# Seven of twelve weight pieces of the second mixer decoded inside its first block, with the pieces in another order

## The chip, the core and the metric

The kernel runs on one core of a Trainium2 chip. The metric is the device time of one execution in microseconds (us). The engines are PE (TensorE, matmuls), PEld (its weight loads), DVE (VectorE), ACT (ScalarE), POOL (GpSimd) and SP (SyncE, which issues the DMAs here). Each runs its own queue in order.

## What is computed

The reference is three steps one after the other. B = 4 sequences, S = 768 positions, 8 heads of 48 (together 384 columns).

```python
# linear attention with a decaying state, per head
for t in range(S):
    cur = einsum('bhd,bhe->bhde', u * k[t], v[t])
    y[t] = einsum('bhd,bhde->bhe', r[t], state + cur)
    state = w * state + einsum('bhd,bhe->bhde', k[t], v[t])
# first mixer: 384 -> 1024 -> 384, a convolution of 3 taps makes the gate
h = maximum(x @ w_in, 0)
conv = conv_w[0] * h[t-1] + conv_w[1] * h[t] + conv_w[2] * h[t+1]
x = (h * sigmoid(conv)) @ w_out
# second mixer: 384 -> 1536 -> 384, with a norm ahead and a residual
xn = (x - mean) / sqrt(var + 1e-6) * g_ln
out = x + maximum(xn @ w_ch1, 0) @ w_ch2
```

## The kernel before

All rows are cut into 24 tiles of 128. Attention makes one tile after the other (generator `attention`, two steps a tile). The first mixer runs in 8 blocks of 384 rows (loop variable j, 0 to 7), each over 8 slices f of 128 of the 1024 inner columns. The second mixer runs in 6 blocks of 512 rows, each over 12 slices f of the 1536. In a slice 9 matmuls make `psm` from the three column groups of the input (high x high, high x low, low x high part of input and weight), and the products with the second matrix go into accumulators `acc`, 9 or 12 matmuls, three slices late (`LAG`). The second mixer takes `rh` (ACT, line 487) and `rl` (DVE, line 488) out of psm, which has two buffers. In the first mixer DVE makes `c` (lines 474 and 455) and `gl` (line 461), and for attention `rk`, `kks`, `av`, `a`, `aT`, `sn`, `sw` and `xl`. Attention's steps are put between the slices by a count, `pace`.

**Weight pieces.** Weights come as words that must be decoded into a high and a low part. A piece is 128 rows by 768 (or 512) columns; `wjob` (line 139) makes a job of it. There are 22 jobs: 0 to 9 are the first mixer's weights, 10 to 21 the second mixer's: six pieces of `w_ch1` (`c1h`, `c1l`, three for each half of 768 columns) and six of `w_ch2` (`c2h`, `c2l`, each for two slices f). A job loads `st` (SP, three buffers), takes the magnitude into `wdec` (ACT, line 75 in the profile) and clamps it (POOL), then has four steps on DVE: a shift, two merges with `st` (SCALAR_TENSOR_TENSOR wdec<-st,wdec), and the low part `c1l` or `c2l`, which needs ACT's copy `c1h` or `c2h`. All these helpers stand at line 75 in the profile. `wdo(count, last)` (line 208) takes that many steps; the fourth step of a job and the first of the next go together, so a job takes three counts. `need(job)` finishes all jobs up to that one.

**What sets the order.** The loops call `wdo` at fixed places: `after1` (line 768) runs twice a slice of the first mixer, `after2` (line 798) once a slice of the second. The jobs run in the order of their making. The program order is then changed by a scheduler that works ahead of time and keeps, on each engine, the decode and all matmuls in program order but may move the others around them. `before2` calls `need` for the pieces which the slice uses. `choose_path` (line 713) loads w and makes a flag `general` on DVE; line 811 reads the flag into a register on every engine.

Of the kernel before, what the change touches and what calls it, by code (L numbers as in the profile page):

```python
# [16 lines left out]
DM = H * D  # L17
# [4 lines left out]
NF2 = FF2 // 128  # L22
# [9 lines left out]
NB = B * BPB  # L32
# [16 lines left out]
def body(ctx, tc, r, k, v, w, u, w_in, conv_w, w_out, g_ln, w_ch1, w_ch2, rkT, krv, small, out):  # L49
# [59 lines left out]
    c2h = [big.tile([128, 2, DM], F32R, name=f"c2h{f}") for f in range(NF2 // 2)]  # L109
    c2l = [big.tile([128, 2, DM], F32R, name=f"c2l{f}") for f in range(NF2 // 2)]  # L110
# [8 lines left out]
    def magnitude(st, n, engine=go):  # L119

        t = ap.tile([128, WN], F32, tag="wd", name="wdec", bufs=2)[:, 0:n]
        ao.activation(out=t, in_=words(st, n)[1].bitcast(F32), func=AF.Abs)
        engine.tensor_scalar(out=t, in0=t, scalar1=W_MIN, scalar2=W_MAX, op0=ALU.max, op1=ALU.min)
        return t
# [14 lines left out]
    def wjob(src, n, hi, lo, scale=None):  # L139

        st, mag = [], []

        def load():
            st.append(io.tile([128, 2 * WN], I32, tag="st", name="st", bufs=3))
            dst = st[0][:, 0:2 * n]
            if len(src.shape) == 3:
                dst = dst.rearrange("p (a n) -> p a n", a=src.shape[1])
            so.dma_start(out=dst, in_=src.bitcast(I32))

        def ahead():  # L150
            if not mag:
                mag.append(magnitude(st[0], n, vo if me < 4 else go))

        def steps():
            ahead()
            t = mag[0]
            yield from decode(st[0], n, t)
            if me + 1 < min(len(wjobs), w_loaded[0]):
                wjobs[me + 1][2]()
            if len(src.shape) == 3:  # L160
                t = t.rearrange("p (a n) -> p a n", a=src.shape[1])
            kw = {} if scale is None else {"scale": gl[:, scale:scale + 1]}
            ao.activation(out=hi, in_=t, func=AF.Copy, **kw)
            yield
            if scale is None:
                vo.tensor_tensor(out=lo, in0=t, in1=hi.bitcast(F32), op=ALU.subtract)
            else:
                vo.scalar_tensor_tensor(out=lo, in0=t, scalar=kw["scale"], in1=hi.bitcast(F32),
                                        op0=ALU.mult, op1=ALU.subtract)
        me = len(wjobs)  # L170
        wjobs.append((load, steps(), ahead))
        return len(wjobs) - 1

    wi_job, wo_job, c1_job, c2_job = {}, {}, {}, {}

    def rows2(w_, f):
        return w_[f * 128:f * 128 + 256, :].rearrange("(a p) d -> p a d", p=128)
# [14 lines left out]
    for f0 in range(0, FF2, WN):  # L192
        for kt in range(KT):
            for f in range(f0 // 128, (f0 + WN) // 128):
                c1_job[f] = len(wjobs)
            wjob(w_ch1[kt * 128:kt * 128 + 128, f0:f0 + WN], WN, c1h[f0 // WN][kt],
                  c1l[f0 // WN][kt], kt)
    for f in range(0, NF2, 2):
        c2_job[f] = c2_job[f + 1] = wjob(rows2(w_ch2, f), 2 * DM, c2h[f // 2], c2l[f // 2])
    w_loaded, w_done = [0], [0]  # L200

    def wload(count):
# [5 lines left out]
    def wdo(count=1, last=None):  # L208

        for _ in range(count):  # L210
            while w_done[0] < (len(wjobs) if last is None else last + 1):
                wload(w_done[0] + 2)
                if next(wjobs[w_done[0]][1], "end") != "end":
                    break
                w_done[0] += 1
# [541 lines left out]
    for j in range(NB):  # L757
        slot = [0]
        while finished[0] < min((j + 1) * TT - (j % 2), NT - 1):
            step()  # L760

        def before1(f):
            if f < NF1:
                need(wi_job[f // 4])
            if f >= LAG - 1:
                need(wo_job[f - LAG + 1])

        def after1(f):
            slot[0] += 1
            pace[0] += 2 if j else 1.9  # L770
            if j == 1:
                pace[0] += 0.4
            if pace[0] >= 5:
                pace[0] -= 5
                step()
            if j == 0:
                wdo(2, wo_job[NF1 - 1])
            elif j < NB - 2:
                wdo(slot[0] % 4 == 0, c1_job[NF2 - 1])
            else:  # L780
                wdo(slot[0] % 3 == 0, c2_job[4])
            if j == NB - 1:
                if slot[0] == 1:
                    ahead[0] = prefetch(0)
                elif slot[0] >= 7:
                    next(ahead[0], None)

        mixer1(xT[j], spill(j), before1, after1)
# [4 lines left out]
    for j in range(NB2):  # L793
        def before2(f):
            need(c1_job[f])
            need(c2_job[max(f - LAG + 1, 0)])

        def after2(f):
            wdo(2)
            if f == 1 and j + 1 < NB2:  # L800
                ahead[0] = prefetch(j + 1)
            elif f >= 4:
                next(ahead[0], None)

        x1s, xn = normed.pop(j)
        mixer2(xn, TT2, lambda acc, x1s=x1s, j=j: finish(
            acc, x1s, lambda t0: rows[j * T2 + t0:j * T2 + t0 + 128, :]), before2, after2)
        for _ in ahead[0]:
            pass
# [70 lines left out]
```

## Time and profile before

| what | value |
|---|---|
| timed runs | 675.46 us median of 3 (673.67 to 676.84) |
| the profiled execution | 671.88 us, span 670.2 us, mean granted clock 0.977 |
| PE busy | 630.2 us, 94% of the span |
| DVE busy | 426.6 us, 64% |
| ACT busy | 263.5 us, 39% |
| POOL busy | 133.8 us, 20% |
| start of the second mixer's first psm | 352.48 us |
| start of the last matmul | 664.04 us |

Times in the profile count from the start of the span. The share of an engine is a mean over the whole span. Waits name what ended last before the waiting instruction could start. The granted clock is a share of TensorE's 2.4 GHz; its other level is 1.2 GHz. A block of the second mixer takes some 50 us.

### The profile page before, as it was taken

How to read it: one execution, taken by the hardware profiler on the slowest of the kernel's cores; microseconds unless marked ns; L12 is line 12 of the kernel's file. 1: busy time of each engine (PE TensorE's matmuls, PEld its weight loads, DVE VectorE, ACT ScalarE, POOL GpSimd, SP SyncE). 2: the span in 40 equal slices, each digit the busy share in tenths (PEclk: the TensorE clock that was granted, in tenths of full speed). 3: DMA queues.
4: the chain of work that ended last, by engine and by line, in shares of the span. 5: the costliest groups of instructions: out<-in, count | busy, mean ns of one | idle time of the engine just before them, and what ended most of it. 6: DMA issues, size and time to landing. Idle time of an engine off the chain costs nothing.

```text
span 670.2 us, 11679 instructions
## 1 busy us (share of the span) xinstructions
PE 630.2 (94%) x4782; PEld 574.5 (86%) x4782; DVE 426.6 (64%) x772; ACT 263.5 (39%) x518; POOL 133.8 (20%) x142
## 2 busy tenths in 40 slices
PE   5979799989899999999999999999999999999996
PEld 4858678879788888999998999999999999999996
DVE  7869999989998999977999522412422422421211
ACT  3457566546464565566774311221111221121110
POOL 6466532312031213211415000100100100100000
PEclk9988899989899998999999999999999999999998
DMA  8655525245235433203043002000200200200101
GB/s 281 193 170 189 176 76 183 85 149 166 78 110 176 141 107 128 84 2 130 5 140 118 0 1 70 25 1 27 68 1 23 72 1 13 83 1 1 47 1 51
DMA packets 25294, 56.50 MB, mean 84 GB/s; under 512 B 2961, under 2 KB 15378, under 8 KB 25234
## 3 DMA queue, kind: packets, MB, share of 16 engines
q1 hardware_dynamic: 25234, 55.68, 26.2%
q8 instruction: 39, 0.64, 0.4%
q14 instruction: 21, 0.17, 0.1%
HBM read 46.24 MB, written 9.44 MB: 83 GB/s over the span
## 4 chain that ended last, share of the span: by engine, by line
PE 67%; DVE 18%; DMA 6%; issue 4%; POOL 2%; ACT 2%; SPq 0%; DVEq 0%; POOLq 0%
PE acc L75 30%; PE psm L75 30%; DMA rk<-in_rkT_dram 5%; DVE c L474 4%; DVE wdec L75 4%; PE yps L75 3%; DVE rk L347 3%; PE dps L75 1%; DVE aT L363 1%; DVE gl L461 1%; DVE c L455 1%; PE pxt L75 1%; POOL wdec L75 1%; DMA x1b<-x_dram 1%; PE pst L75 0%
## 5 line engine op out<-in xcount | busy, mean ns | idle before, releaser
L488 DVE SCALAR_TENSOR_TENSOR rl<-psm,rh 128x512 fp32r<-128x512 f32 x72 | 49.5, 688 | 141.2 <-ACT rh L487 141.2
L487 ACT ACTIVATE rh<-psm 128x512 fp32r<-128x512 f32 x72 | 43.1, 598 | 202.6 <-PE psm L75 202.6
L75 PE MATMUL acc<-c2l,rh 128*128 128x384 f32 x288 | 97.1, 337 | 0.0
L75 PE MATMUL acc<-c2h,rl 128*128 128x384 f32 x288 | 97.0, 337 | 0.0
L75 PE MATMUL acc<-c2h,rh 128*128 128x384 f32 x288 | 96.9, 336 | 0.0
L75 PE MATMUL psm<-xnh,c1h 128*128 128x512 f32 x216 | 86.6, 401 | 0.0
L474 DVE SCALAR_TENSOR_TENSOR c<-h,tables,c 128x384 f32<-128x384 f32 x128 | 83.9, 661 | 3.8 <-ACT c L472 3.2
L75 PE MATMUL psm<-xnh,c1l 128*128 128x512 f32 x216 | 85.0, 394 | 0.0
L75 PE MATMUL psm<-xnl,c1h 128*128 128x512 f32 x216 | 84.7, 392 | 0.0
L75 PE MATMUL acc<-woh,gl 128*128 128x384 f32 x192 | 66.8, 348 | 7.5 <-DVE gl L461 7.5
L75 PE MATMUL psm<-xh,wih 128*128 128x386 f32 x192 | 69.0, 359 | 4.1 <-DVE aT L363 2.7
L75 PE MATMUL acc<-wol,gh 128*128 128x384 f32 x192 | 66.0, 344 | 3.9 <-DVE wol L75 3.9
L75 PE MATMUL acc<-woh,gh 128*128 128x384 f32 x192 | 68.0, 354 | 1.4 <-ACT x L496 1.3
L75 PE MATMUL psm<-xl,wih 128*128 128x386 f32 x192 | 67.0, 349 | 2.4 <-POOL xl L288 2.4
L75 PE MATMUL psm<-xh,wil 128*128 128x386 f32 x192 | 67.2, 350 | 1.7 <-DVE wil L75 1.7
L75 POOL TENSOR_SCALAR wdec<-wdec 128x768 f32<-128x768 f32 (+2 forms) x19 | 53.7, 2825 | 74.7 <-ACT wdec L75 70.1
L511 POOL TENSOR_TENSOR rs<-rs,nhalf 128x1 f32<-128x1 f32 x24 | 18.4, 772 | 214.1 <-DVE rs L510 201.7
L75 PEld LDWEIGHTS acc<-c2l,rh 128*128 128x128 f32 x288 | 54.1, 188 | 3.0
L75 PEld LDWEIGHTS acc<-c2h,rh 128*128 128x128 f32 x288 | 54.1, 188 | 2.8
L75 PEld LDWEIGHTS acc<-c2h,rl 128*128 128x128 f32 x288 | 54.1, 188 | 0.0
L460 ACT ACTIVATE gh<-c 128x384 fp32r<-128x384 f32 x64 | 33.3, 523 | 39.7 <-DVE c L455 39.3
L75 PEld LDWEIGHTS psm<-xnh,c1l 128*128 128x128 f32 x216 | 40.6, 188 | 9.2
(115 smaller groups left out, 1128.3 us busy)
## 6 DMA issues: line engine op xcount, KB each, us to landing
rk<-in_rkT_dram SPq DMA_DIRECT2D x24, 448.0 KB, 4.6
st<-in_moe_w_ch_dram SPq DMA_DIRECT2D x12, 768.0 KB, 5.8
rv<-in_krv_dram SPq DMA_DIRECT2D x18, 448.0 KB, 4.7
kt<-in_krv_dram SPq DMA_DIRECT2D x24, 192.0 KB, 2.6
x_dram<-x SPq DMA_DIRECT2D x24, 192.0 KB, 2.0
x1b<-x_dram SPq DMA_DIRECT2D x24, 192.0 KB, 3.7
out_dram<-x1b SPq DMA_DIRECT2D x24, 192.0 KB, 2.3
st<-in_moe_w_in_dram SPq DMA_DIRECT2D x6, 512.0 KB, 7.0
```

The lines of the kernel that those rows point to most:

```text
L75: return lambda *args, **kw: tc.keep_in_program_order(op(*args, **kw))
L347: v_.tensor_tensor(out=rk, in0=rk, in1=trk, op=ALU.mult)
L363: v_.copy_predicated(out=aT[:, q], mask=later.bitcast(I32).unsqueeze(1).to_broadcast([128, NP, C]), data=dps[q])
L455: v_.tensor_tensor(out=st["c"], in0=st["h"][:, 1:T + 1], in1=st["c"], op=ALU.mult)
L460: a_.activation(out=st["gh"], in_=st["c"], func=AF.Copy)
L461: v_.tensor_tensor(out=st["gl"], in0=st["c"], in1=st["gh"].bitcast(F32), op=ALU.subtract)
L474: v_.scalar_tensor_tensor(out=c, in0=h[:, o:o + T], scalar=cw[:, tap, f:f + 1], in1=c, op0=ALU.mult, op1=ALU.add)
L487: a_.activation(out=gh[:, 0:cols], in_=ps[:, 0:cols], func=AF.Relu)
L488: v_.scalar_tensor_tensor(out=gl_[:, 0:cols], in0=ps[:, 0:cols], scalar=0.0, in1=gh[:, 0:cols].bitcast(F32), op0=ALU.max, op1=ALU.subtract)
L511: g_.tensor_tensor(out=rs[:, 1:2], in0=rs[:, 0:1], in1=nhalf, op=ALU.pow)
```

## The change

The pieces are made in the order first half of w_ch1 (3), first two pieces of w_ch2, second half of w_ch1 (3), last four pieces of w_ch2. Up to now the order was w_ch1 (6), then w_ch2 (6). In the first mixer, blocks 1 to 7 take one step at every fifth call, up to the second piece of w_ch2 (job 14). Before, blocks 1 to 5 took one at every fourth call, up to the last piece of w_ch1 (job 15), and blocks 6 and 7 one at every third, up to job 18. In the second mixer three steps a slice are taken in place of two.

```diff
@@ -195,8 +195,8 @@
                 c1_job[f] = len(wjobs)
             wjob(w_ch1[kt * 128:kt * 128 + 128, f0:f0 + WN], WN, c1h[f0 // WN][kt],
                   c1l[f0 // WN][kt], kt)
-    for f in range(0, NF2, 2):
-        c2_job[f] = c2_job[f + 1] = wjob(rows2(w_ch2, f), 2 * DM, c2h[f // 2], c2l[f // 2])
+        for f in ((0, 2) if f0 == 0 else range(4, NF2, 2)):
+            c2_job[f] = c2_job[f + 1] = wjob(rows2(w_ch2, f), 2 * DM, c2h[f // 2], c2l[f // 2])
     w_loaded, w_done = [0], [0]
 
     def wload(count):
@@ -775,10 +775,8 @@
                 step()
             if j == 0:
                 wdo(2, wo_job[NF1 - 1])
-            elif j < NB - 2:
-                wdo(slot[0] % 4 == 0, c1_job[NF2 - 1])
             else:
-                wdo(slot[0] % 3 == 0, c2_job[4])
+                wdo(slot[0] % 5 == 0, c2_job[3])
             if j == NB - 1:
                 if slot[0] == 1:
                     ahead[0] = prefetch(0)
@@ -796,7 +794,7 @@
             need(c2_job[max(f - LAG + 1, 0)])
 
         def after2(f):
-            wdo(2)
+            wdo(3)
             if f == 1 and j + 1 < NB2:
                 ahead[0] = prefetch(j + 1)
             elif f >= 4:
```

The order on DVE in the first mixer, third block (j = 2), before, from the decode merge that started at 163.05 us to the gl that started at 169.62:

```order
L75 SCALAR_TENSOR_TENSOR wdec<-st,wdec 128x768
L474 SCALAR_TENSOR_TENSOR c<-h,tables,c 128x384
L372 TENSOR_TENSOR xl<-yps,xh 128x3x128
L363 COPY_PREDICATED aT<-tables,dps 128x512 x2
L455 TENSOR_TENSOR c<-h,c 128x384
L75 SCALAR_TENSOR_TENSOR c1l_104<-wdec,smallt,c1h_98 128x768
L455 TENSOR_TENSOR c<-h,c 128x384
L75 TENSOR_SCALAR wdec<-wdec 128x768
L393 TENSOR_TENSOR sn<-pst,sw 112x192
L249 TENSOR_TENSOR kks<-kt,tables 128x16x48
L461 TENSOR_TENSOR gl<-c,gh 128x384
```

The same place in the changed kernel:

```order
L474 SCALAR_TENSOR_TENSOR c<-h,tables,c 128x384
L372 TENSOR_TENSOR xl<-yps,xh 128x3x128
L455 TENSOR_TENSOR c<-h,c 128x384
L363 COPY_PREDICATED aT<-tables,dps 128x512 x2
L75 SCALAR_TENSOR_TENSOR wdec<-st,wdec 128x768
L455 TENSOR_TENSOR c<-h,c 128x384
L461 TENSOR_TENSOR gl<-c,gh 128x384
L393 TENSOR_TENSOR sn<-pst,sw 112x192
L249 TENSOR_TENSOR kks<-kt,tables 128x16x48
```

The low part and the shift are no longer between the masked copies (COPY_PREDICATED) and the first gl, and sn and kks come behind it.

The order on DVE in the first block of the second mixer, before, from the shift that started at 371.82 us:

```order
L75 TENSOR_SCALAR wdec<-wdec 128x768
L488 SCALAR_TENSOR_TENSOR rl<-psm,rh 128x512
L75 SCALAR_TENSOR_TENSOR wdec<-st,wdec 128x768 x2
L488 SCALAR_TENSOR_TENSOR rl<-psm,rh 128x512
L75 TENSOR_TENSOR c2l_120<-wdec,c2h_114 128x768
L513 TENSOR_SCALAR xn<-x1b,mv,rs 128x384
L431 TENSOR_TENSOR xnl<-pxt,xnh 128x3x128
L488 SCALAR_TENSOR_TENSOR rl<-psm,rh 128x512
```

In the changed kernel, from the read of the flag (line 809 there) on:

```order
L809 TENSOR_LOAD general
L431 TENSOR_TENSOR xnl<-pxt,xnh 128x3x128
L75 TENSOR_TENSOR c2l_117<-wdec,c2h_111 128x768
L75 TENSOR_SCALAR wdec<-wdec 128x768
L488 SCALAR_TENSOR_TENSOR rl<-psm,rh 128x512
L75 SCALAR_TENSOR_TENSOR wdec<-st,wdec 128x768
L513 TENSOR_SCALAR xn<-x1b,mv,rs 128x384
L431 TENSOR_TENSOR xnl<-pxt,xnh 128x3x128
L75 SCALAR_TENSOR_TENSOR wdec<-st,wdec 128x768
L488 SCALAR_TENSOR_TENSOR rl<-psm,rh 128x512
L75 TENSOR_TENSOR c2l_118<-wdec,c2h_112 128x768
L75 TENSOR_SCALAR wdec<-wdec 128x768
```

There the last of the pieces (c2l_120) is done after six rl; now three pieces (to c2l_120) are still open after the seventh, and the read of the flag stands in the block where before it stood behind the last store.

On PE the matmuls stand in the same order in both kernels. The read of the flag moved from behind the last matmul to this place, ahead of the seventh psm (f = 6) of the second mixer's first block:

```order
L75 MATMUL acc_4334<-c2l_116,rh 128x384
L75 MATMUL acc_4334<-c2h_110,rl 128x384
L75 MATMUL pxt<-tables,xn 128x128
L809 TENSOR_LOAD general
L75 MATMUL pxt<-tables,xn 128x128 x2
```

Ahead of it stand the first of the three transposes of a tile of the next block, and behind it the other two.

## Rows read from the trace of the kernel before

**Rows 1.** Windows: us, busy of PE, PEld, DVE, ACT, POOL (instructions), PEclk, DMA share, GB/s.

```profile
107.00:275.00 168.00, 155.98 (x1675) 141.10 (x1677) 159.48 (x265) 91.64 (x191) 38.58 (x36) 0.97 0.41 125
275.00:352.00 77.00, 75.80 (x584) 73.13 (x574) 66.72 (x128) 54.41 (x109) 18.61 (x11) 1.00 0.24 77
352.00:403.00 51.00, 51.00 (x262) 46.14 (x261) 28.99 (x57) 16.17 (x28) 10.45 (x6) 1.00 0.10 39
```

**Rows 2.** Windows, decode tile wdec alone: us, busy of DVE, ACT, POOL, then clock and DMA.

```profile
107.00:275.00 168.00, 20.33 (x22) 9.09 (x10) 15.88 (x5) 0.97 0.41 125
275.00:352.00 77.00, 11.64 (x13) 6.98 (x8) 11.17 (x4) 1.00 0.24 77
352.00:403.00 51.00, 11.53 (x13) 4.34 (x5) 6.79 (x2) 1.00 0.10 39
```

**Rows 3.** Waits of PE, 107 to 275 us: total us, times, longest.

```profile
PE acc L75 <- DVE gl L461: 6.3, 5, 2.9
PE psm L75 <- DVE aT L363: 2.7, 2, 1.6
PE pst L75 <- DVE xl L372: 1.4, 2, 0.9
```

**Rows 4.** Timeline of PE: start, us, instruction, [idle before it <- releaser].

```profile
143.42 0.44 PE L75 MATMUL acc<-woh,gl 128*128 128x384 f32 x1 [2.86 <-DVE gl L461]
...
170.21 0.44 PE L75 MATMUL acc<-woh,gl 128*128 128x384 f32 x1 [2.26 <-DVE gl L461]
...
222.09 0.44 PE L75 MATMUL acc<-woh,gl 128*128 128x384 f32 x1 [0.56 <-DVE gl L461]
...
230.58 0.67 PE L75 MATMUL pst<-rv,kks 128*64 128x48 f32 x16 [0.88 <-DVE xl L372]
...
351.00 0.44 PE L75 MATMUL acc<-woh,gl 128*128 128x384 f32 x1 [0.74 <-DVE gl L461]
```

**Rows 5.** Windows of 5 us behind the two longest stalls, columns as in rows 1.

```profile
145.00:150.00 5.00, 5.00 (x77) 4.33 (x77) 3.55 (x7) 2.36 (x5) 1.09 (x1) 0.72 0.43 103
170.00:175.00 5.00, 4.79 (x65) 4.15 (x67) 5.00 (x11) 1.74 (x4) 0.01 (x1) 0.67 0.29 76
```

**Rows 6.** Timeline of DVE ahead of the matmul that started at 170.21.

```profile
163.05 0.94 DVE L75 SCALAR_TENSOR_TENSOR wdec<-st,wdec 128x768 int32<-128x768 int32 x1
163.92 0.60 DVE L474 SCALAR_TENSOR_TENSOR c<-h,tables,c 128x384 f32<-128x384 f32 x1
...
166.62 1.00 DVE L75 SCALAR_TENSOR_TENSOR c1l<-wdec,smallt,c1h 128x768 fp32r<-128x768 f32 x1
...
168.01 0.55 DVE L75 TENSOR_SCALAR wdec<-wdec 128x768 int32<-128x768 int32 x1
...
169.62 0.54 DVE L461 TENSOR_TENSOR gl<-c,gh 128x384 fp32r<-128x384 f32 x1
```

**Rows 7.** Chain that ended last, second mixer's first block: start, us, what.

```profile
365.49 2.09 PE acc L75 x12
367.57 2.07 PE psm L75 x9
...
402.26 2.06 PE psm L75 x9
```

**Rows 8.** Timelines of POOL (first row) and DVE, second mixer's first block.

```profile
367.35 2.77 POOL L75 TENSOR_SCALAR wdec<-wdec 128x768 f32<-128x768 f32 x1
...
367.48 1.50 DVE L75 SCALAR_TENSOR_TENSOR wdec<-st,wdec 128x768 int32<-128x768 int32 x1
...
370.95 0.96 DVE L75 TENSOR_TENSOR c2l<-wdec,c2h 128x768 fp32r<-128x768 f32 x1 [0.97 <-ACT c2h L75]
```

**Rows 9.** Reads of the flag, line 811: min/median/max ns, first and last start.

```profile
L811 PEldq TENSOR_LOAD <-general x1: 488/488/488, 661.1 to 661.1; - x1
...
L811 DVEq TENSOR_LOAD <-general x1: 791/791/791, 664.4 to 664.4; - x1
```

**Rows 10.** Waits of DVE, 107 to 275 us.

```profile
DVE rk L347 <- DMA rk<-in_rkT_dram: 6.1, 7, 1.7
```

## The prediction

> **What bounds the kernel now.** I began with the busy windows by stage, since a share over the whole span mixes stages with different limits. Times of the trace are microseconds from the span's start. In the first mixer with attention beside it, 107 to 275, the reader is to see two engines close to full at once: DVE is busy 159.48 of 168.0 us and PE 155.98 [rows 1]. From 275 to 352, where attention runs out, PE has 75.80 of 77.0 and DVE 66.72. In the first block of the second mixer, 352 to 403, PE is busy all 51.0 us and DVE only 28.99 [rows 1]. So an operation of DVE costs most in the first stage and least in the third. The decode there takes 20.33 us of DVE in 22 operations, 11.64 in 13 and 11.53 in 13 [rows 2].
>
> Next the waits of PE: between 107 and 275 it lost 6.3 us to gl, 2.7 to aT and 1.4 to xl, all made by DVE, 10.4 us together [rows 3]. The timeline shows the waits singly [rows 4]: 2.86 and 2.26 us for gl are the longest. Behind each the granted clock was below full, 0.72 and 0.67 of 2.4 GHz over 5 us [rows 5], which is work lost of 5 x 0.28 = 1.4 and 5 x 0.33 = 1.65 us. The DVE timeline ahead of the second shows why gl was late: a c1l and a shift of the decode stand in the queue in front of it [rows 6].
>
> **The change, part by part.** A piece's decode is four DVE operations: shift, two merges, low part. With the starts of successive operations as their cost, a merge takes 163.92 - 163.05 = 0.87 us [rows 6]; by their durations the low part is 1.00 and the shift 0.55, some 0.08 less by starts, so 0.92 and 0.47. By the order, 15 decode operations stand between the reduces of the attention tiles that ran at 102 and at 275, where there were 22; then 5 instead of 13; then 28 instead of 13. The sum, 48, is the same: work is moved and none is removed.
>
> *First mixer, 107 to 275.* Seven operations fewer are 7 x 20.33/22 = 6.5 us of DVE. That is the upper bound for relief alone, if DVE held PE all the time; the lower bound is nothing, or a loss where an operation lands ahead of something urgent. I go by stalls, with the order:
> - 170.21: ahead of gl the change has one merge and no low part, shift, sn or kks. By the row the gl started 169.62 - 166.62 = 3.0 us after c1l began, of which 0.47 is the c between them: 2.5 us less, more than the 2.26 waited. All of it goes.
> - 143.42: c1l, shift and av leave, a merge comes (0.92 + 0.47 + 0.47 - 0.87 = 1.0), and one merge (0.87) is gone earlier: 1.9 of 2.86.
> - 222.09 (0.56) has one merge fewer ahead, 230.58 (0.88) has lost its c1l and shift: both go [rows 4].
> - The gain is given back in part in the tile after 238, where c1l, shift and a merge now stand ahead of the masked copies that make aT. Bounds: 0 and 2.26 us; I take 1.4, the two that are new there.
>
> Together 1.9 + 2.26 + 0.56 + 0.88 - 1.4 = 4.2 us. The clock: what was at the lower level may come back, 0 to 3.05 us [rows 5]. I take 1.65, that of the stall which goes whole. The stage: 5.85 us, under the 6.5 of relief for its DVE part.
>
> *First mixer, 275 to 352.* PE idled 77.0 - 75.80 = 1.2 us there, 0.74 of it at 351.00 behind gl [rows 1, 4]. Three pieces leave this stage, also two merges ahead of that gl. Bounds 0 and 1.2; I take 0.8.
>
> *Second mixer, first block.* 15 more operations at 11.53/13 are 13.3 us of DVE. POOL's clamp of a piece takes 2.77 us and the merge beside it took 1.50 instead of 0.94 [rows 6, 8]: 0.56 each, and six clamps stand in the block instead of two, so 2.2 us. The flag's read, which the order puts into this block, holds DVE 0.79 [rows 9]. 28.99 + 13.3 + 2.2 + 0.8 = 45.3 of 51.0 us: it fits, and PE hides it. If the cover fails, PE pays each microsecond. What is due when: psm has two buffers, so block f+2 waits for rl of f. At a pace of 2.07 + 2.09 per f [rows 7], walking DVE's queue row by row, with up to 0.97 us for ACT's copy ahead of a low part [rows 8], I get rl of f = 10 done near 400.5 where the first matmul of the next block wants it at 402.26 [rows 7]; c2l of the fourth of the seven pieces near 382, where its use starts at 383. So little is left at f = 7 to 10. Bounds for the lateness: 0 and about 3 us; I take 0.5, as both estimates still meet their times. PE's own read of the flag takes 0.488 us [rows 9] between two transposes; 0 to 0.5, I take 0.5, since PE has no other gap here.
>
> Loads: SP issues the last four pieces' loads in this block instead of late in the first mixer, the last three behind its flag read, which waits for DVE's write of the flag early in the block. By the order this write comes before the third rl, some 25 us before those pieces are needed, so I cost the loads at nothing; their cover is that lead. The x1b loads of the second block no longer stand behind a load that waits for a buffer, which helps only DVE where it has room. PE's order is otherwise the same. ACT's and POOL's operations move with the pieces; both have room (16.17 and 10.45 of 51 us) [rows 1]. At the end DVE's read at 664.4 [rows 9] lay beside the output stores: no gain.
>
> **Sum.** -5.85 - 0.8 + 0.5 + 0.5 = -5.65 us. The profiled execution took 671.88 us (span 670.2), below all three timed runs, so from it I get 666.2; against the median of 675.46 I forecast **669.9 us**, 0.8% less.
>
> **Contention weighed.** Row first: beside a clamp of 2.77 us a merge was longer by 0.56 us [rows 6, 8], and the sum uses that. The Trainium skill, page "SBUF — State Buffer", section "Who interferes with whom", says that a DVE instruction with two SBUF inputs and a GpSimd instruction that reads SBUF take the shared ports as an exclusive lock, so that the second one blocks fully. By that rule a clamp could cost DVE 2.77 us each. The merge of 1.50 us started 0.13 us after the clamp and ended before it, so the trace does not bear it out for this pair.
>
> **Rivals.**
> 1. *The relief is taken back.* DVE waited 6.1 us in seven waits for rk's loads [rows 10], and those loads wait for buffers that PE frees. Where rk comes last, fewer decode operations only lengthen DVE's wait. Then perhaps a third of the 5.85 us stays: 675.46 - 2.0 = 673.5. For it: rows 10. Against it: the two longest stalls wait for gl, with decode directly ahead.
> 2. *DVE becomes the bound of the second mixer's first block*, which is slower. Place: rl of f = 7 to 10 behind decode. It decides from the point where DVE is over 1.8 us later than my walk (402.26 - 400.5); beyond that PE pays one for one. If each of the six clamps held DVE for its 2.77 us, not 0.56, that would be 13.3 us more, 11.5 past the slack: 669.9 + 11.5 - 0.5 = about 681. Against it: 45.3 of 51 us, and the merge of rows 8. By the section named above this is what the page's rule would give. For it: the fast pace of decode, one piece per f, is shown nowhere in this trace for more than three pieces.
> 3. *More than the sum.* With both clock dips gone and nothing given back near 240 the first stage gives 4.2 + 1.4 + 3.05 = 8.65, the second 1.2: 675.46 - 9.85 + 0.5 = 666.1.
>
> That the move does not take place is excluded by the order: 28 decode rows stand after the first rl.
>
> **How the numbers follow.** Forecast 0.50, rival 1 0.30, rival 2 0.13, rival 3 0.07. A measurement of this kernel tells about 0.5% from no change, 3.4 us. Faster by more: most of the forecast (0.45), rival 3 (0.07), a little of rival 1 (0.04): 0.56. Slower by more: rival 2 (0.13). The rest 0.31. The forecast alone spans 666.5 to 673, its runs' spread and the unknown bounds of 1.4, 1.65 and 3 us included. For 8 in 10, from rival 3 with half a percent of slack below, 664.5, over rival 1 with some loss in the block, to 677.0.
>
> **What would show it.** Right: no PE wait over 2 us for gl between 107 and 275, waits for DVE there down from 10.4 to about 6 us, at most one or two low-clock windows; DVE near 45 of 51 us in the first block of the second mixer with PE without a gap over 1 us; the first rl earlier by 6 to 7 us. Wrong: the same sum of PE waits at other places with rk's waits grown (rival 1), or PE waits for rl or c2l in that block (rival 2).

## The result and the profile after

| | before | after |
|---|---|---|
| median of timed runs | 675.46 us (7 runs, 672.02 to 676.84) | 668.53 us (7 runs, 665.23 to 671.08) |
| the profiled execution | 671.88 us, span 670.2 | 668.53 us, span 666.8 |
| mean granted clock | 0.977 | 0.976 |

The changed kernel is faster: ratio 0.9894, 95% interval [0.9861, 0.9927], 6.9 us by the medians. The forecast was 669.9.

The busy windows of the changed kernel by stage, columns as in [rows 1]. The borders lie 3 us earlier than in [rows 1], since the second mixer starts that much earlier:

```profile
104.00:272.00 168.00, 158.94 (x1708) 144.45 (x1710) 160.44 (x266) 93.69 (x193) 39.14 (x36) 0.98 0.40 126
272.00:349.00 77.00, 76.36 (x595) 74.31 (x586) 63.01 (x125) 50.45 (x106) 7.50 (x8) 1.00 0.19 65
349.00:400.00 51.00, 51.00 (x262) 46.02 (x262) 39.92 (x68) 22.71 (x36) 23.51 (x10) 1.00 0.24 74
```

The same windows for the decode tile wdec alone, columns as in [rows 2]:

```profile
104.00:272.00 168.00, 13.21 (x15) 7.18 (x8) 12.21 (x4) 0.98 0.40 126
272.00:349.00 77.00, 4.28 (x5) 1.78 (x2) 3.27 (x1) 1.00 0.19 65
349.00:400.00 51.00, 24.55 (x28) 11.63 (x13) 19.95 (x6) 1.00 0.24 74
```

The operations stand where the order said: 15, 5 and 28 on DVE. In the first stage PE is busy 158.94 us where it was 155.98, 3.0 us longer in the same 168 us. DVE is as full as before (160.44): the room that the decode left was filled by the work that had waited behind it. In the third window DVE took 10.9 us more (39.92 against 28.99), and PE still has no gap in 51.0 us.

PE's waits in the first stage, to be read against [rows 3] (total us, times, longest):

```profile
PE psm L75 <- DVE aT L363: 3.2, 2, 1.8
PE acc L75 <- ACT x L496: 2.7, 2, 2.3
PE acc L75 <- DVE gl L461: 1.8, 2, 1.6
PE pst L75 <- DVE xl L372: 1.1, 2, 0.9
```

In the kernel before, the same window (107 to 275 us) has this row for x:

```profile
PE acc L75 <- ACT x L496: 1.3, 2, 1.0
```

The waits for gl fell from 6.3 us in five to 1.8 in two. The waits for aT, where the relief was to be given back, rose from 2.7 to 3.2, and those for x, ACT's copy of an accumulator, from 1.3 to 2.7. DVE's own waits for rk's loads fell from 6.1 us in seven [rows 10] to 4.3 in three:

```profile
DVE rk L347 <- DMA rk<-in_rkT_dram: 4.3, 3, 1.8
```

Singly, on PE's timeline:

```profile
144.69 0.44 PE L75 MATMUL acc<-woh,gl 128*128 128x384 f32 x1 [1.57 <-DVE gl L461]
...
194.14 0.44 PE L75 MATMUL acc<-woh,gh 128*128 128x384 f32 x1 [2.32 <-ACT x L496]
...
229.17 0.69 PE L75 MATMUL psm<-xh,wih 128*128 128x386 f32 x1 [1.78 <-DVE aT L363]
```

A fourth stall, for aT at 254.82, is 1.39 us long; before has one of 1.10 there. The stalls of [rows 4] at 170.21, 222.09 and 351.00 have no counterpart, and the one at 143.42 lost 1.3 of its 2.86 us. In place of the one for xl at 230.58, just ahead of a slice's psm, the change has the longer one for aT at 229.17, ahead of the same psm. After 279 us PE waits nowhere in the first mixer.

The stall at 194 ends with ACT, but DVE stands behind it. In ACT's queue x comes after a gh that waits for DVE's c:

```profile
192.16 0.52 ACT L460 ACTIVATE gh<-c 128x384 fp32r<-128x384 f32 x1 [2.15 <-DVE c L455]
...
193.62 0.47 ACT L496 ACTIVATE x<-acc 128x384 f32<-128x384 f32 x1
```

The clock was low in these windows behind the stalls at 194 and 229:

```profile
195.00:200.00 5.00, 4.72 (x68) 4.03 (x70) 4.96 (x10) 2.73 (x7) 0.18 (x1) 0.66 0.56 166
...
230.00:235.00 5.00, 5.00 (x23) 5.00 (x22) 4.92 (x9) 2.92 (x7) 0.00 (x0) 0.75 0.26 78
```

**Where the time came from.** PE's matmuls stand in the same order in both kernels, so the first matmul of the same psm group can be compared, group by group. At the second slice of the first mixer's second block both kernels have run the same program, yet before starts it at 100.07 us and after at 102.53. These 2.46 us are a difference of two executions and none of the change. With that start taken off, the table gives the start of a group minus the start in the trace of before (worked out from the timelines; negative is earlier). The other columns are experiments told below, by their headings; "two steps" is the change with two counts a slice in the second mixer, "eight, ahead" has clamps two pieces ahead.

| group starts in before at | after | two steps | late stage | into blocks 6, 7 | none early | eight | nine | eight, ahead | order alone |
|---|---|---|---|---|---|---|---|---|---|
| 176.0 | -6.5 | -6.6 | -0.3 | -7.0 | -5.5 | -6.9 | -6.1 | -6.8 | -3.6 |
| 183.3 | -6.2 | -6.3 | 0.4 | -6.7 | -4.0 | -6.6 | -5.9 | -6.5 | -2.5 |
| 201.2 | -3.0 | -3.6 | 1.1 | -3.7 | -5.5 | -3.3 | -2.9 | -4.7 | -1.9 |
| 226.3 | -5.5 | -6.1 | 0.4 | -6.2 | -3.9 | -5.8 | -5.4 | -7.2 | -2.3 |
| 243.9 | -3.0 | -4.9 | 0.8 | -5.2 | -3.6 | -3.3 | -3.4 | -5.4 | -1.9 |
| 256.0 | -3.6 | -5.8 | 0.3 | -6.0 | -4.5 | -4.1 | -4.6 | -6.3 | -2.4 |
| 266.9 | -5.2 | -7.4 | -1.2 | -7.6 | -6.0 | -5.6 | -6.2 | -7.8 | -4.0 |
| 284.1 | -4.0 | -6.2 | -0.1 | -6.4 | -5.6 | -5.0 | -6.0 | -7.1 | -2.9 |
| 314.3 | -4.0 | -6.2 | 0.0 | -6.4 | -4.3 | -4.9 | -6.0 | -7.1 | -2.9 |
| 352.3, second mixer | -5.8 | -7.8 | -1.9 | 0.5 | -2.4 | -6.9 | -7.8 | -9.0 | -2.6 |
| 371.6, f = 5 | -5.8 | -7.8 | -1.9 | 0.5 | -2.4 | -6.9 | -7.9 | -9.0 | -2.6 |
| 402.1, second block | -5.7 | -7.8 | -1.9 | 0.5 | -2.5 | -2.9 | 3.5 | -2.5 | -2.6 |
| 653.8, near the end | -5.9 | -7.7 | -1.8 | 0.4 | -2.1 | -2.9 | 3.3 | -2.4 | -2.6 |

So the change wins 6.2 us by 183, gives 3.2 of it back by 244, stands at 4.0 at 284 and wins 1.8 more up to the second mixer; after that it neither wins nor loses anything. The 3.2 us go in two places, at the stall for x (183 to 201) and at the stall for aT (226 to 244); between them a stall for aT that before has at 206.88 (1.61 us) is gone.

Three columns show how fine such a reading may be. "Two steps" has the same DVE order in the first mixer, and its trace differs by 2 us from 244 to 284. "Order alone" wins nothing by its median (675.78 us), but its traced execution was the fastest of its twelve (670.42) and reads 2.6 us earlier here. And every column wins 1.6 us between 256 and 267, "late stage" too: that is the trace of before, whose clock was low there, behind its stall for aT at 255.96:

```profile
255.00:260.00 5.00, 4.04 (x15) 4.04 (x16) 5.00 (x10) 2.69 (x6) 3.10 (x3) 0.70 0.02 8
```

One traced execution can't tell less than 2 to 3 us by stage. The medians, with 1.1 to 2.2 us to either side in their intervals, are finer, but tell no stages.

### The profile page after: what moved, and what is told of

Same layout as the page of the kernel before. It is cut to its first block, busy times and chain, and to the rows that moved or that the text cites. A ratio compares the mean times of both kernels' runs of the same rounds, so it can differ in the third digit from the quotient of the medians.

```text
span 666.8 us, 11692 instructions
## 1 busy us (share of the span) xinstructions
PE 629.3 (94%) x4782; PEld 574.1 (86%) x4782; DVE 431.7 (65%) x772; ACT 264.3 (40%) x518; POOL 135.1 (20%) x142
## 4 chain that ended last, share of the span: by engine, by line
PE 62%; DVE 24%; DMA 6%; issue 3%; ACT 3%; POOL 1%; SPq 1%; DVEq 0%; ACTq 0%
PE psm L75 30%; PE acc L75 30%; DVE c L474 6%; DMA rk<-in_rkT_dram 5%; DVE wdec L75 4%; DVE c L455 2%; DVE aT L363 2%; DVE rk L347 2%; DVE gl L461 2%; PE yps L75 1%; PE pxt L75 1%; DVE av L352 1%; DVE kks L249 1%; DVE a L354 1%; DVE xl L372 1%
## 5 line engine op out<-in xcount | busy, mean ns | idle before, releaser
L474 DVE SCALAR_TENSOR_TENSOR c<-h,tables,c 128x384 f32<-128x384 f32 x128 | 87.0, 685 | 7.4 <-ACT c L472 6.8
L75 POOL TENSOR_SCALAR wdec<-wdec 128x768 f32<-128x768 f32 (+2 forms) x19 | 55.3, 2911 | 50.8 <-ACT wdec L75 41.3
L511 POOL TENSOR_TENSOR rs<-rs,nhalf 128x1 f32<-128x1 f32 x24 | 15.5, 654 | 230.5 <-DVE rs L510 229.9
L454 ACT ACTIVATE c<-c 128x384 f32<-128x384 f32 x64 | 33.4, 521 | 44.0 <-DVE c L474 43.5
L357 POOL TENSOR_SCALAR_AFFINE_SELECT aT<-a 128x1024 f32<-128x1024 f32 x18 | 29.1, 1617 | 104.0 <-PE yps L75 45.1
```

Source lines behind the costliest of these rows:

```text
L75: return lambda *args, **kw: tc.keep_in_program_order(op(*args, **kw))
L357: g_.affine_select(out=aT.rearrange("x q p c -> x (q p) c"), in_=a8.to_broadcast([128, H, C]), compare_op=ALU.is_equal, fill=0.0, base=0, ...
L454: a_.activation(out=st["c"], in_=st["c"], func=AF.Sigmoid)
L474: v_.scalar_tensor_tensor(out=c, in0=h[:, o:o + T], scalar=cw[:, tap, f:f + 1], in1=c, op0=ALU.mult, op1=ALU.add)
L511: g_.tensor_tensor(out=rs[:, 1:2], in0=rs[:, 0:1], in1=nhalf, op=ALU.pow)
```

## The experiments

Diffs are against the changed kernel. Where a text speaks of theory A, it is the prediction's: decode taken off DVE in the early first mixer ends PE's waits there, and the free DVE of the second mixer's first block takes it up. Ratios are to the kernel before, with 95% intervals.

**The order of the pieces alone.** The new order with the old pace.

```diff
-            else:
-                wdo(slot[0] % 5 == 0, c2_job[3])
+            elif j < NB - 2:
+                wdo(slot[0] % 4 == 0, 15)
+            else:
+                wdo(slot[0] % 3 == 0, 18)
...
-            wdo(3)
+            wdo(2)
```

> The pieces in the new order, decoded at the old pace (nine in the first mixer, three in the second mixer's first block). Theory A (the gain is DVE work taken out of 107 to 275 us): no operation leaves that stage, so the ratio to before is 0.995 to 1.005. Theory B (the gain comes from the new arrangement of the queues, whatever the amount of work): 0.988 to 0.993.

Measured: 675.78 us, 1.0005 [0.9983, 1.0026]. The order alone does nothing. PE's waits for gl, 95 to 360 us, are as long as in the kernel before in the same window (second row):

```profile
PE acc L75 <- DVE gl L461: 7.3, 7, 2.9
```

```profile
PE acc L75 <- DVE gl L461: 7.5, 7, 2.9
```

**Only the late part.** Blocks 1 to 5 keep the old pace up to job 15, blocks 6 and 7 decode nothing, the rest goes into the second mixer.

```diff
-            else:
-                wdo(slot[0] % 5 == 0, c2_job[3])
+            elif j < NB - 2:
+                wdo(slot[0] % 4 == 0, 15)
```

> New order, blocks 1 to 5 of the first mixer at the old pace, nothing decoded in its blocks 6 and 7, six pieces in the second mixer's first block. Theory A: only the last stage of the first mixer is relieved, where PE idled 1.2 us; ratio 0.997 to 1.001. Theory B, or a theory that the second half of the first mixer gave the gain: 0.988 to 0.993.

Measured: 672.88 us, 0.9971 [0.995, 0.9993], 2.0 us (0.5 to 3.4 by the interval). In the rows of the table it stays within 1.2 us of before up to 314 us and is level there; then 1.9 us are won up to the second mixer. The change wins the same 1.8 there, and the other kernels of the table that decode little or nothing in blocks 6 and 7 win 1.6 to 2.0. So the late first mixer is worth about 1.9 us, where the prediction had 0.8. The early part is the rest, some 5 of the 6.9 us; this is a difference of medians, since the early part can't be run without a place for its decode.

**Only the early part.** Blocks 1 to 5 at the new pace, and the decode that is saved there goes into blocks 6 and 7 instead of the second mixer.

```diff
-            else:
+            elif j < NB - 2:
                 wdo(slot[0] % 5 == 0, c2_job[3])
+            else:
+                wdo(slot[0] % 2 == 0, 18)
...
-            wdo(3)
+            wdo(2)
```

> New order, blocks 1 to 5 as in the change (every fifth call, five pieces), four more pieces at every second call of blocks 6 and 7, three pieces in the second mixer's first block as before. Theory A: DVE's relief in 107 to 275 us is kept, so most of the gain is too, ratio 0.990 to 0.995, less where blocks 6 and 7 get 16 decode operations (14 us of DVE) and PE begins to wait there. If the gain needs the free DVE of the second mixer's first block, 0.997 to 1.003.

Measured: 676.23 us, 1.0019 [1.0002, 1.0035]: a miss, no gain at all. The table shows why: the relief is there in full at 314 us (-6.4) and is gone at 352 (+0.5). On PE's timeline of this kernel stand five stalls in 11 us, three of them shown, where the timeline of before has two in the whole late stage:

```profile
316.49 0.44 PE L75 MATMUL acc<-woh,gl 128*128 128x384 f32 x1 [0.75 <-DVE gl L461]
...
325.70 0.44 PE L75 MATMUL acc<-woh,gh 128*128 128x384 f32 x1 [0.97 <-ACT gh L460]
327.47 0.69 PE L75 MATMUL acc<-woh,gl 128*128 128x384 f32 x1 [1.15 <-DVE gl L461]
```

So the late first mixer is not free either. It looked free by its share: DVE was busy 66.72 of 77.0 us there [rows 1]. At this pace, a step at every second call, the gain needs the one stage whose DVE really is free; a slower pace into blocks 6 and 7 was not run.

**No early decode at all.** Blocks 1 to 4 decode nothing, blocks 5 to 7 all up to job 14.

```diff
-            else:
-                wdo(slot[0] % 5 == 0, c2_job[3])
+            elif j >= 5:
+                wdo(slot[0] % 2 == 0, c2_job[3])
```

> No decode of the second mixer's pieces in blocks 1 to 4 of the first mixer, five pieces in blocks 5 to 7, seven in the second mixer's first block as in the change. Doubles the suspected relief: 15 more decode operations, 13 us of DVE, leave the stage before 275 us. Theory A: PE's waits for DVE there (some 7 us left with the change) fall by half or more, ratio to before 0.980 to 0.986 (3 to 6 us under the change). Rival (what is left are waits for the rk loads and in the chain of attention, which less decode does not shorten): within 1.5 us of the change, 0.987 to 0.992.

Measured: 671.28 us, 0.994 [0.9918, 0.9961]: short of what both theories gave, though the interval still touches the rival's range. At 267 us, where its decode begins, it is 6.0 us earlier than before, no better than the change (5.2) and its twin with two steps (7.4); what follows in blocks 5 to 7 costs it 3.6 us of that. PE's waits, 95 to 360 us, moved to another product of DVE:

```profile
PE psm L75 <- DVE aT L363: 7.8, 5, 2.5
PE acc L75 <- DVE gl L461: 2.9, 2, 1.7
```

In its stage DVE itself still waits for rk's loads, 100 to 270 us, as in [rows 10]:

```profile
DVE rk L347 <- DMA rk<-in_rkT_dram: 6.4, 7, 1.7
```

In three of PE's five stalls for aT the rk ahead of the masked copies had waited for its load, 1.73, 1.05 and 0.53 us; the first of them on DVE's timeline, whose aT PE waited for at 177.94 (1.40 us):

```profile
176.03 1.22 DVE L347 TENSOR_TENSOR rk<-rk,tables 112x1024 f32<-112x1024 f32 x1 [1.73 <-DMA rk<-in_rkT_dram]
```

So the relief saturates: after the first third of the decode is gone, what holds PE is more and more attention's own chain (loads of rk, masked copies, aT), and taking the other two thirds away bought nothing that this trace shows up to 267 us. That is the mechanism of rival 1, setting in later than the rival supposed. The median alone can't show it, since this kernel also decodes at a faster pace in blocks 5 to 7.

**Two steps a slice in the second mixer.** `wdo(3)` back to `wdo(2)`.

```diff
-            wdo(3)
+            wdo(2)
```

> The change with two decode steps a slice in the second mixer, as before, not three; seven pieces still fall into its first block. With three steps the last rl that could hold PE there was 4.9 us early, so if DVE has this much room the pace does not matter: ratio 0.988 to 0.991 as the change, no PE wait in that block. If the third step is what keeps the pieces in time (c2l of the fourth piece was 2.7 us early), 0.992 to 0.998 with PE waits for c1l or c2l.

Measured: 668.25 us, 0.9899 [0.9866, 0.9932], the same as the change. `need` finishes in time what the count leaves open, so the third step is no part of the gain.

**Another phase of the same pace.** The step falls on the second of five calls.

```diff
-                wdo(slot[0] % 5 == 0, c2_job[3])
+                wdo(slot[0] % 5 == 2, c2_job[3])
```

> The change with its decode calls in the first mixer shifted by two of five (second, seventh, twelfth call of a block): the same work, in other places of DVE's queue. If the amount of DVE work in the stage decides, 0.987 to 0.992, as the change. If it matters more which operation stands ahead of which gl, xl or aT, PE's waits move, and the ratio may lie anywhere from 0.982 to 0.998, with the difference in blocks 1 to 4.

Measured: 669.83 us, 0.9923 [0.9893, 0.9953]. Its interval overlaps the change's. In its trace one wait for gl of 2.6 us appears, so that the place of single operations shifts stalls about; the medians don't tell it from the change.

**Eight pieces and nine pieces in the first block.** The first mixer stops at job 13, or at job 12.

```diff
-                wdo(slot[0] % 5 == 0, c2_job[3])
+                wdo(slot[0] % 5 == 0, c2_job[1])
```

> Eight pieces in the second mixer's first block, four in the first mixer at the change's pace, so its blocks 6 and 7 decode nothing. DVE in the second mixer's first block: 39.9 + 3.5 = 43.4 us of 51. If that fits (the last rl 4.9 us early, less some 4): ratio 0.986 to 0.990, the end of the first mixer 0 to 0.7 us sooner than with the change. If DVE becomes the bound there: PE waits for rl and 0.991 to 0.996.

```diff
-                wdo(slot[0] % 5 == 0, c2_job[3])
+                wdo(slot[0] % 5 == 0, c1_job[0])
```

> Nine pieces there, three in the first mixer. The piece of w_ch2 that the first slices use must be finished before the first slice, so its steps stand together at the head of the block. DVE: 39.9 + 7 = 47 us of 51. The theory that DVE bounds the block from some point says that this is past it: rl late by 3 to 8 us, PE waits of that size, ratio 0.992 to 1.002. If it still fits, 0.986 to 0.990.

Measured: eight 669.57 us, 0.9909 [0.9876, 0.9942]; nine 678.29 us, 1.0046 [1.0025, 1.0066]. The median of eight lies between the two ranges expected for it and does not tell it from the change; what follows is read from its trace, the slowest of its six runs (671.08). The first mixer is won again, 6.9 and 7.8 us by the table, but now the second mixer's first block pays: 4.0 us with eight, 11.4 with nine. PE waits for c1h and c1l there, not for rl as was expected. Its stalls with eight:

```profile
373.92 0.50 PE L75 MATMUL psm<-xnh,c1h 128*128 128x512 f32 x1 [1.20 <-ACT c1h L75]
374.97 0.50 PE L75 MATMUL psm<-xnh,c1l 128*128 128x512 f32 x1 [0.32 <-DVE c1l L75]
```

with this window behind them:

```profile
374.00:379.00 5.00, 4.68 (x16) 4.10 (x17) 4.30 (x6) 1.42 (x2) 3.04 (x1) 0.67 0.58 155
```

The waits are 1.52 us and the clock at 0.67 takes some 5 x 0.33 = 1.65 more, 3.2 of the 4.0. With nine pieces two longer waits follow one another:

```profile
371.45 0.90 PE L75 MATMUL pxt<-tables,xn 128*128 128x128 f32 x3 [2.48 <-DVE xn L513]
...
379.35 0.80 PE L75 MATMUL psm<-xnh,c1h 128*128 128x512 f32 x1 [3.40 <-ACT c1h L75]
```

The second half of w_ch1 is due at f = 6. With nine the loads have a part in it too: SP issues the next block's x1b only at 360.77 us, behind st loads, and the wait of 2.48 us is for the norm made from it. Over the whole block DVE with eight pieces still has room, 43.14 of 51.0 us busy:

```profile
347.40:398.40 51.00, 49.41 (x242) 43.71 (x241) 43.14 (x71) 23.80 (x37) 27.74 (x11) 0.97 0.29 89
```

This made me suspect the chain of a piece (magnitude on ACT, clamp on POOL, DVE, copy on ACT) with its two wdec buffers.

**Clamps two pieces ahead.** Three wdec buffers, and from the second half of w_ch1 on a piece's load, magnitude and clamp are issued one piece earlier; with eight, seven and nine pieces.

```diff
-        t = ap.tile([128, WN], F32, tag="wd", name="wdec", bufs=2)[:, 0:n]
+        t = ap.tile([128, WN], F32, tag="wd", name="wdec", bufs=3)[:, 0:n]
...
-            if me + 1 < min(len(wjobs), w_loaded[0]):
-                wjobs[me + 1][2]()
+            for nxt in [i for i in range(me + 1, me + (3 if me > 13 else 2)) if i < min(len(wjobs), w_loaded[0])]:
+                wjobs[nxt][2]()
...
-                wload(w_done[0] + 2)
+                wload(w_done[0] + (3 if w_done[0] > 13 else 2))
```

> Eight pieces stay for the first block, as in the kernel with eight, but from the second half of w_ch1 on three wdec buffers let the magnitude and clamp of a piece run two pieces ahead, and its load is issued one piece earlier. Chain theory (magnitude, clamp, four DVE steps and ACT's copy of successive pieces hang on one another, 5.5 to 6 us a piece, and that and not the load of DVE made the second half of w_ch1 late): PE's waits for c1h and c1l at f = 6 (1.5 us and the clock behind them) go, the 3.6 us lost there come back, and the ratio to the kernel before falls from 0.991 to 0.984 to 0.988. Rival (DVE's own queue in the block, with more in front of rl and the low parts): the loss at f = 6 stays at 3 us or more, ratio 0.989 to 0.995.

> The change as it is, seven pieces, with the same three wdec buffers and clamps two pieces ahead. Chain theory: the change lost nothing in the second mixer, so there is nothing to win there, 0.988 to 0.992. Rival (the chain costs something in the late first mixer too, where the change still lost 0.5 us and more): 0.984 to 0.987.

> Nine pieces for the first block, with three wdec buffers and clamps two pieces ahead. With nine pieces in the block and two buffers the loss at f = 4 to 6 was 11.4 us. Chain theory: most of it comes back, since the first mixer of that kernel was the fastest of all (7.9 us less); ratio 0.984 to 0.992. Rival (the loads: the x1b loads of the next block stand behind loads of st on SP that wait for buffers, and the transposes wait for xn): PE's wait for xn stays and the ratio is 0.998 or more.

Measured: eight 673.34 us, 0.9969 [0.9944, 0.9994]; seven 671.43 us, 0.9934 [0.9909, 0.9959]; nine 679.32 us, 1.0057 [1.0026, 1.0087]. None is better than its twin without it: the times that the chain theory gave did not come, and those of eight and seven lie above both ranges expected. With eight pieces the loss between f = 4 and the second block grew from 4.0 to 6.5 us. The third piece of the second half again, on PE:

```profile
374.03 0.79 PE L75 MATMUL psm<-xnh,c1h 128*128 128x512 f32 x1 [3.24 <-ACT c1h L75]
```

On DVE the low parts of that kernel start at 361.88, 367.79 and 374.01 us: a piece still takes 5.9 to 6.2 us. With eight pieces and two buffers it was nearly the same, 5.8 and 6.0, and the rows between two low parts show what fills it:

```profile
368.06 1.02 DVE L75 SCALAR_TENSOR_TENSOR c1l<-wdec,smallt,c1h 128x768 fp32r<-128x768 f32 x1 [1.01 <-ACT c1h L75]
368.99 0.56 DVE L75 TENSOR_SCALAR wdec<-wdec 128x768 int32<-128x768 int32 x1
369.57 0.69 DVE L488 SCALAR_TENSOR_TENSOR rl<-psm,rh 128x512 fp32r<-128x512 f32 x1
370.18 0.95 DVE L75 SCALAR_TENSOR_TENSOR wdec<-st,wdec 128x768 int32<-128x768 int32 x1
371.05 0.98 DVE L513 TENSOR_SCALAR xn<-x1b,mv,rs 128x384 f32<-128x384 f32 x1
371.95 0.95 DVE L75 SCALAR_TENSOR_TENSOR wdec<-st,wdec 128x768 int32<-128x768 int32 x1
372.82 0.55 DVE L431 TENSOR_TENSOR xnl<-pxt,xnh 128x384 fp32r<-128x384 f32 x1
373.90 1.02 DVE L75 SCALAR_TENSOR_TENSOR c1l<-wdec,smallt,c1h 128x768 fp32r<-128x768 f32 x1 [0.54 <-ACT c1h L75]
```

No row waits for POOL. DVE's own queue makes the pace: four decode operations, the rl of the slice, a tile of the next block's norm, and the wait for ACT's copy, one piece in about 6 us, while PE takes a slice in about 4.2 us [rows 7]. But DVE is not full and does not simply fall behind from slice to slice: in the same trace the rl at 361.22 and 365.49 waited 0.87 and 0.91 us for ACT's rh, so there DVE had caught up with PE. By these rows the fixed order of the queue, with its waits for ACT, sets when a piece is done, and not the sum of DVE's work alone. With eight pieces the third low part of the second half starts 26.5 us after the block's first matmul (373.90 from 347.42), in the change 21.1 us after it (370.05 from 348.99); PE begins the slice that needs it after 23.7. That is rival 2 in another form: its place is f = 6 and not 7 to 10, and DVE has idle time when it is late. Whether another order would take the eighth piece was not run.

The look-ahead also changed something that I had not meant. The loads of st and of x1b stand in one queue on SP, and the third st load now waits for its buffer in front of the x1b loads. SP's issues with eight pieces, without and with the look-ahead (start, us, what):

```profile
337.87 2.67 SPq L744 DMA_DIRECT2D x1b<-x_dram  x4
```

```profile
330.74 22.98 SPq L75 DMA_DIRECT2D st<-in_moe_w_ch_dram  x3
353.82 1.80 SPq L744 DMA_DIRECT2D x1b<-x_dram  x4
```

So the loads for the norm of the next block, which in the change (338.86) and with eight pieces go out late in the first mixer, came 16 us later, and the norm came into the busiest part of DVE's queue. How much of the 2.5 us lost against the twin comes from that and whether the look-ahead alone would help was not separated, so this run is no clean test of the chain theory; the DVE rows above, without a wait for POOL, speak against its part with the clamps and buffers. With nine pieces and the look-ahead the same queue decides: x1b is issued at 369.29 and PE waits for the norm.

```profile
369.29 1.84 SPq L744 DMA_DIRECT2D x1b<-x_dram  x4
```

```profile
379.14 0.90 PE L75 MATMUL pxt<-tables,xn 128*128 128x128 f32 x3 [7.14 <-DVE xn L513]
```

No version ran clearly better than the change (two steps, 668.25 us, is the same). Of those tried, seven pieces is the most that the first block takes without a stall of PE.

## Why the prediction was right, and where its terms were off

The sum was -5.65 us from the profiled execution and 669.9 us in all (675.46 - 5.65 is 669.8); the result is 668.53, and by the groups -5.8 us past the first 100 us. The direction, the stage and the mechanism came as forecast: the stalls for gl with decode directly ahead went, and the first block of the second mixer took the decode in. That -5.65 and -5.8 lie so close is in part luck: in this trace the early first mixer gave 1.9 us less than its term (-4.0 at 284 against -5.85, and 1.6 of the 4.0 are the low clock in the trace of before), and the late one 1.0 and the second mixer 1.0 more than theirs. Term by term:

- *First mixer, early, -5.85.* The walk by stalls holds up to 176 us: 1.9 + 2.26 and 1.65 for the clock are 5.8, and the trace gives -6.5. The gl stall at 170 is gone, as the order said. Without the early part the rest is worth 2.0 us. PE's waits for DVE in the rows above fell from 10.4 to 6.1 us, where about 6 were foreseen; with x, which waits for DVE at second hand, they fell from 11.7 to 8.8.
- *Given back near 240, 1.4.* This term failed in place and cause. The decode stands ahead of the masked copies there as the prediction says (c1l at 236.12, shift at 237.05, merge at 239.83 us on DVE), but PE waits nowhere from 230 to 254. From 183 to 244 the change lost 3.2 us at the stall for x at 194.14, won 2.5 by 226 and lost 2.5 again at the stall for aT at 229.17, where the 0.88 of 230.58 was to go and did not. Ahead of both DVE had run no decode for 6 and 18 us (the last ended at 185.44 and 210.67). So it is not decode in a worse place but attention's and the mixer's own chain through DVE, which is nearer to rival 1 than to this term. The stalls brought low clock with them, 0.66 and 0.75; the twin with two steps has both, with the clock at 1.00 behind the second, and gives back 1.4.
- *The stall at 143, 1.9 of 2.86 gone.* It is 1.57 us, so 1.3 are gone. Its clock came back too, which the sum had left out, 1.00 against 0.72 [rows 5]:

```profile
145.00:150.00 5.00, 5.00 (x85) 4.43 (x84) 4.94 (x9) 2.49 (x6) 1.19 (x1) 1.00 0.38 111
```

- *First mixer, late, -0.8.* This term was mis-sized: -1.8 in the change, -1.9 when done alone. I counted only PE's idle time between 275 and 352, and took the bound of 1.2 us from it. Idle time is counted from the modelled end of the matmul before, but undisturbed matmuls there start 0.18 us apart and last 0.34, and the one behind a stall takes longer too. By the starts in the trace of before, three places where gl came late lost 0.7, 0.2 and 1.0 us (at 323.17, 326.51 and 351.00), 1.9 together. Around the last, with the stall of [rows 4] between the two rows:

```profile
349.93 0.33 PE L75 MATMUL acc<-wol,gh 128*128 128x384 f32 x1
...
351.28 0.34 PE L75 MATMUL acc<-woh,gh 128*128 128x384 f32 x1
```

  These two starts lie 1.35 us apart, where 0.35 is the pace: 1.0 lost, with an idle time of 0.74.
- *Second mixer's first block, +1.0.* It cost nothing: the offset is -5.8 at its start and at its end. DVE is busy 39.92 us, not 45.3. Of the 5.4 us between, 2.5 are decode: the 28 operations took 24.55 us where I had 11.53 + 13.3 + 2.2 = 27.0, so the 2.2 us for clamps did not come. 2.1 are other work: 39.92 - 24.55 = 15.4 us against 28.99 - 11.53 = 17.5 before. The norm of the next block is in that: its x1b loads went out at 349.98 us before, behind an st load that waited for its buffer, and at 338.86 in the change, so that its statistics are made ahead of the block. The prediction saw this and gave it nothing. And 0.8 is the flag's read, which the busy time does not count (it took DVE 0.54 us here). The rl of f = 10 was done at 394.06 us and due at the next block's first matmul at 398.82: 4.8 us in hand where I walked 1.8.
- *PE's read of the flag, +0.5.* It costs nothing that can be seen. The trace books it at 373.7 us, and the matmuls of the psm around that time start 0.23 us apart as elsewhere:

```profile
L809 PEldq TENSOR_LOAD <-general x1: 486/486/486, 373.7 to 373.7; - x1
```

- *Contention of clamp and merge, 0.56 for each clamp.* A merge that started with a clamp took 1.59 us, where others take 0.95, and the clamp of 2.77 us went on beside it:

```profile
372.00 2.77 POOL L75 TENSOR_SCALAR wdec<-wdec 128x768 f32<-128x768 f32 x1 [2.19 <-ACT wdec L75]
```

```profile
372.05 1.59 DVE L75 SCALAR_TENSOR_TENSOR wdec<-st,wdec 128x768 int32<-128x768 int32 x1
```

That is 0.64 us longer, near the 0.56 of [rows 8], and not the whole 2.77. Most merges were not longer at all: of seven that lay wholly beside a clamp in this block five took 0.94 to 0.97 us, such as the one below beside a clamp that ran from 352.74 for 5.01 us (spans of POOL are rough); a merge of 1.30 us at 383.67 also started close behind a clamp's start.

```profile
353.68 0.97 DVE L75 SCALAR_TENSOR_TENSOR wdec<-st,wdec 128x768 int32<-128x768 int32 x1
```

So a price for every clamp was too much. By the Trainium skill, page "SBUF — State Buffer", section "Who interferes with whom", the two would shut one another out for a whole instruction. Here again the trace does not agree.

Rival 1 did not decide the change, since DVE's waits for rk fell (6.1 to 4.3 us), but it is real behind it: with no early decode at all PE waits 7.8 us for aT and nothing more is won. Rival 2 is real from the eighth piece on. Rival 3's time, 666.1, lies 2.4 us under the median. What the prediction lacked is how near rival 2 was: a piece takes DVE about 6 us in that block and PE needs 4.2 for a slice, and one more piece costs 4.0 us there in its trace. Of the signs that the prediction named, PE's waits and clock came as named; DVE in that block (39.92 us, not near 45) and the first rl (352.15 against 357.85, 5.7 us earlier, not 6 to 7) did not. The walk of DVE's queue had its tightest point at f = 7 to 10; it lies at the due time of the second half of w_ch1, f = 6, where in the change the third low part ended at 371.07 us and the slice that uses it last began at 372.66.

Also, before's profiled execution was faster than its median by 3.6 us (671.88 against 675.46), after's was at it. Taking the sum from the profiled execution and setting it on the median as a difference, as the prediction did, served here, since the 2.46 us by which before was ahead at 100 us are none of the change; the two profiled times by themselves differ by only 3.35 us.

## What to carry to other kernels

Background work moves well out of a stage where two engines are full together, but only into a stage where the engine that does it is free; a stage that was 87% full took it all back at the pace tried, as blocks 6 and 7 did. Judge the receiving stage by what is due when in the in-order queue and by the pace per item against the pace of the consumer, not by the busy share over the stage: with eight pieces DVE was busy 43 of 51 us, and the eighth piece was late all the same. And when a load is issued earlier, look at what stands behind it in the same queue.

## What the runs showed of the hardware that was not expected

- Two executions of the same program part differ by 1 to 4 us at 100 us of the span (offsets of 0.95 to 3.83 us over twelve kernels whose first 100 us are the same or nearly so), and the same DVE order gave -4.0 and -6.2 us at 284. The kernel with the order alone, no faster by its median, read 2.6 us earlier. Readings of single traces by stage are no finer than that.
- Stalls of 1.5 us together cost about as much again by the clock, 0.67 in the 5 us behind them with eight pieces. But this does not follow every stall: behind the 1.57 us at 144.69 in the change the clock was 1.00, and behind the 1.78 us for aT it was 0.75 in the change and 1.00 in its twin with two steps (230 to 235 us in both). Behind the stall of 3.24 us the granted clock was at its lower level for a whole window:

```profile
375.00:380.00 5.00, 5.00 (x17) 4.72 (x17) 3.98 (x6) 2.38 (x3) 2.11 (x2) 0.50 0.46 145
```

This window is of the kernel with eight pieces and the look-ahead: PE is busy all 5 us and gets through 17 matmuls, where the same kernel does 28 in the window from 385 to 390 at full clock.

```profile
385.00:390.00 5.00, 5.00 (x28) 4.49 (x27) 4.41 (x6) 2.18 (x4) 2.25 (x1) 1.00 0.00 0
```
